# q, k and v of an attention kernel loaded in two transfers each: rows of 1024 and 2048 floats, and the remainders

## The chip, the cores and the metric

The kernel runs on one core of a Trainium2 chip. The metric is device time in microseconds of one launch, as the median of several runs; lower is better.

## The reference

Three layers follow each other: an attention with two sparse masks, a mixture of experts in which 8 experts take 288 tokens each by greedy choice, and a dense block with an elu. Cut to what matters:

```python
def _attn_ref(q, k, v):                       # q, k, v: (4, 8, 576, 64)
    scores = np.matmul(q, k.transpose(0, 1, 3, 2)) / np.sqrt(64)
    rel = pos[:, None] - pos[None, :]         # pos = arange(576)
    mask_local = (rel >= 0) & (rel < 32)
    mask_strided = (rel >= 0) & (pos[None, :] % 32 == pos[:, None] % 32)
    ...                                       # heads 0 to 3 local, 4 to 7 strided
    return np.matmul(softmax(scores), v)

def _moe_ref(x, w_gate, w1, w2):              # x: (2304, 512)
    # the largest logits first, each token to one expert, each expert 288 tokens
    out[mask] = np.maximum(x[mask] @ w1[e], 0) @ w2[e]

def _moe2_ref(x, w_in, w_out):                # w_in, w_out: float64
    return elu(x @ w_in) @ w_out
```

## The kernel before

The host part, `layout`, brings the inputs into the order in which they are loaded. Heads and batches are grouped to 8 units of 1152 queries, and both kinds of mask become blocks of 32 queries by 64 keys.

`attention` goes over the units. For unit u, `load_k` loads `kt` (the transposed keys, with 32 zero columns ahead) in two transfers of 64 partitions each into `kd`, one half for each of two heads, and `qt` in one transfer of 128 partitions; `load_v` loads `vb` in two transfers of 32 partitions into `vd`. `kd`, `vd`, `qt` and the output `os` have two buffers each, so the loads of unit u+2 can start only when unit u has been read, and the output of unit u+2 can be written only when that of unit u is stored. The other halves of `kd` and `vd` are zero (`zero`), so that one matmul works for two heads.

Each unit has three steps. TensorE (PE) computes scores (`s_step`), transposes (`t_step`), multiplies with v (`v_step`), transposes again (`x_step`), and at the end of a unit computes routing logits (`l_step`). VectorE (DVE) and ScalarE (ACT) do the softmax. `store` writes a unit's output to `x_d` in DRAM in four transfers with rows of 512 bytes; the experts gather their tokens from there.

Beside the attention runs the preparation of the dense weights (`Dense.slice`): 16 slices, each loaded as 1 MB of float64 words (`in_wd`), and taken apart by ACT, DVE and GpSimd (POOL).

All loads and stores named so far are issued by SyncE (SP), in program order. That order, and the order of each engine's work, comes from a planner, `Line`, which keeps estimated clocks while the program is written. `line.dma(bytes)` charges a transfer 520 ns of queue time and its bytes at 360 a nanosecond; the result says from when on work that needs it is written, and a dense slice is written in only when the DMA clock is less than 2 us ahead (`DMA_AHEAD`).

After the attention the routing finds the tokens of the first expert, a chain on DVE and PE. Then eight experts, each followed by the dense block, keep PE occupied to the end.

Of the kernel before, what the change touches and what calls it, by code (L numbers as in the profile page):

```python
# [36 lines left out]
ORDER = [0, 1, 2, 3, 4, 5, 6, 9, 10, 11, 12, 7, 8, 13, 14, 15]  # L37


# ---------------------------------------------------------------- host layout  # L40
def layout(inp):
    out = {}

    def rows(a):
        a = a.reshape(B, 2, 2, 2, S, D).transpose(0, 1, 3, 2, 4, 5)
        loc = a[:, 0]
        strided = a[:, 1].reshape(B, 2, 2, 18, 32, D).transpose(0, 1, 2, 4, 3, 5).reshape(B, 2, 2, S, D)
        return np.stack([loc, strided], 1).reshape(8, 2, 2 * S, D)

    qr, kr, vr = rows(inp['q']), rows(inp['k']), rows(inp['v'])  # L50
    out['qt'] = np.ascontiguousarray(qr.transpose(0, 1, 3, 2).reshape(8, 128, 4, 3, 96).transpose(0, 1, 3, 2, 4)).reshape(8, 128, 1152)
    kt = np.zeros((8, 2, D, 1184), np.float32)
    kt[..., 32:] = kr.transpose(0, 1, 3, 2)
    out['kt'] = kt.reshape(8, 128, 1184)
    vb = np.ones((8, 2, 32, 36, 65), np.float32)
    vb[..., :64] = vr.reshape(8, 2, 36, 32, D).transpose(0, 1, 3, 2, 4)
    out['vb'] = vb

    low = np.float32(-8e9)
    masks = np.zeros((128, 2, 9, 64), np.float32)  # L60
    qq, kk = np.arange(32)[:, None], np.arange(64)[None, :]
    for j in range(4):
        for i in range(9):
            b18 = (9 * j + i) % 18
            rk, rq = 32 * b18 - 32 + kk, 32 * b18 + qq
            near = (rk >= 0) & (rq >= rk) & (rq - rk < 32)
            same = (rk >= 0) & (rq >= rk) & (rq // 18 == rk // 18)
            masks[32 * j:32 * j + 32, 0, i] = np.where(near, 0, low)
            masks[32 * j:32 * j + 32, 1, i] = np.where(same, 0, low)
    out['mask'] = masks.astype(ml_dtypes.bfloat16)  # L70

    p, c = np.arange(128)[:, None], np.arange(18)[None]
    flat = 128 * (c // 2) + p
    n = 288 * (c % 2) + flat % 288
    t = 576 * (flat // 288) + 32 * (n % 18) + n // 18
    r = 576 * (flat // 288) + n
    out['tokp'] = np.stack([r // 128, r % 128, t // 128, t % 128], -1).astype(ml_dtypes.bfloat16)
    row = np.zeros((128, 16), np.float32)
    row[:, 0:3] = np.arange(3)
    row[:, 8:16] = 8 - np.arange(8)  # L80
    out['rowc'] = row.astype(ml_dtypes.bfloat16)
    out['ufull'] = np.broadcast_to(np.arange(96, dtype=np.float32)[None, :, None],
                                   (128, 96, 18)).astype(ml_dtypes.bfloat16)
    q = np.arange(128)
    out['tri'] = np.stack([q[:, None] <= q[None], np.ones((128, 128))], 1).astype(np.float32).astype(ml_dtypes.bfloat16)

    w1 = inp['moe_w1'].reshape(8, 4, 128, 8, 128).transpose(0, 3, 2, 1, 4).reshape(8, 8, 128, 512)
    w2 = inp['moe_w2'].reshape(8, 8, 128, 512)
    out['we'] = np.ascontiguousarray(np.concatenate([w1, w2], -1)).reshape(64, 128, 1024)
    wi = inp['moe2_w_in'].reshape(4, 128, 16, 128).transpose(2, 1, 0, 3).reshape(16, 128, 512)  # L90
    wo = inp['moe2_w_out'].reshape(16, 128, 512)
    out['wd'] = np.ascontiguousarray(np.concatenate([wi, wo], -1)).view(np.int64)
    out['wg'] = np.pad(inp['moe_w_gate'].reshape(4, 128, 8).transpose(1, 0, 2), ((0, 0), (0, 0), (0, 24)))
    return out


# ---------------------------------------------------------------- estimated clocks that order the work of the engines
class Line:
    """The tensor engine's program drives an estimated clock; jobs (generators that yield the time of their next piece)
    emit the other engines' work at the estimated time when its operands are there, so that no in-order queue blocks."""  # L100
    LAT = 190

    def __init__(self):
# [61 lines left out]
            self.step(40)  # L165

    def idle(self, eng, cost):
        """Whether the engine is idle and no job that it is urgent for is about to want it."""
        u = min([j[1] for j in self.jobs if eng in j[3]], default=1e18)
        return self.free[eng] <= self.now + 80 and not (self.calm and eng != 'pool') and u > self.now + cost - SLACK  # L170

# [2 lines left out]
            yield max(self.now + 40, min(self.free[eng], self.now + 400))  # L174

    def either(self, n):
        """GpSimd or the vector engine for n columns of a two-operand operation, whichever has room."""
        while True:
            if self.free['pool'] <= self.now + POOL_AHEAD and not self.quiet:
                return 'pool'  # L180
# [3 lines left out]


class Bank:
    """One PSUM bank that several jobs share."""

    def __init__(self, pool, line):
        self.pool, self.line, self.taken, self.at = pool, line, False, 0  # L190
# [8 lines left out]
        self.taken, self.at = False, at  # L199


# ---------------------------------------------------------------- dense weights: float64 words to two float32r parts
class Dense:
    """The 16 slices of the hidden dimension, [128, 512] of w_in and [128, 512] of w_out each, as high and low part:
    RES stay on chip in tiles of their own, as many as there are workers in the workers' tiles, the rest goes as float32
    words by DRAM."""

    def __init__(self, nc, I, dr, pool, early, line):
        self.nc, self.I, self.early, self.late, self.line = nc, I, early, None, line
# [14 lines left out]
        self.left -= 1  # L224

    def slice(self, f, k):
        """Float32 words from the float64 ones, then their high and low part."""
        nc, line = self.nc, self.line
        w = self.pool.tile([128, 2048], U32, name="w64", tag=f"w{k}")
        even, odd = w[:, 0::2], w[:, 1::2].bitcast(F32)  # L230
# [50 lines left out]
        t = 0  # L281
# [10 lines left out]
        self.gfree.append(gk)  # L292

    def keep(self):
        """One more slice stays, in the tiles that the float32 words are worked out in."""
        hi, lo = (self.pool.tile([128, 1024], F32R, name="kept", tag=f"g{x}") for x in range(2))
        self.kept = [(hi[:, 512 * n:512 * n + 512], lo[:, 512 * n:512 * n + 512]) for n in range(2)]


# ---------------------------------------------------------------- attention  # L300
def attention(nc, tc, I, x_d, lg, identf, identb, R, line):
    with ExitStack() as ctx:
        cp = ctx.enter_context(tc.tile_pool(name="ac", bufs=1))
# [7 lines left out]
        def load_k(u):  # L311
            qt = wp.tile([128, 1152], F32, name="qt")
            kd = kd_b[u % 2]
            for x in range(2):
                nc.sync.dma_start(kd[64 * x:64 * x + 64, x, :], I['kt'][u, 64 * x:64 * x + 64])
                line.dma(303104)
            nc.sync.dma_start(qt, I['qt'][u])
            U[u] = dict(qt=qt, kd=kd, tk=line.dma(589824))

        def load_v(u):  # L320
            vd = vd_b[u % 2]
            for x in range(2):
                nc.sync.dma_start(vd[64 * x + 32:64 * x + 64, x, 1:37], I['vb'][u, x])
                t = line.dma(299520)
            U[u].update(vd=vd, tv=[])
            line.add(windows(u, vd, t), 0)

# [20 lines left out]
        def zero(engine, eng, tiles, i, lower):  # L348
            for x in range(2):
# [2 lines left out]
                line.put(eng[x] if isinstance(eng, list) else eng, 1240 if not lower else 2070)  # L352
                if lower:
                    engine.memset(tiles[i][64 * x + 32:64 * x + 64, x, 0], 0.0)

        zero([nc.vector, nc.gpsimd], ['dve', 'pool'], kd_b, 0, False)
        load_k(0)
# [222 lines left out]
        line.finish(last)  # L580


# ---------------------------------------------------------------- greedy routing, one expert filled per phase
COLUMNS = ('lm', 'm', 'eq', 'a8', 'oh', 's', 'w', 'cur', 'cd', 'inE', 'sl', 'x1', 't12', 'u', 'V', 'vp')


class Router:
# [47 lines left out]
        self.line.dve(c1 - c0)  # L635

    def prelude(self, p, c0, c1):
        """Of the tokens in the columns c0 to c1: the best open expert, one-hot, and the digits of its logit."""
        t, line, v, D = self.t, self.line, self.nc.vector, self.line.dve
        n = c1 - c0  # L640
        e8 = self.e8[:, None, :].to_broadcast([128, n, 8])
# [38 lines left out]
        yield e  # L680

    def phase(self, p, res, bank, then=None):
        """Fills res['eidx'] ([1,1] int32, the expert that is filled) and res['idx'] ([96,3,2] int32, their
        rows of x and their tokens)."""
        nc, t, line, n = self.nc, {k: x[:, :self.n] if k in COLUMNS else x for k, x in self.t.items()}, self.line, self.n
        v, D = nc.vector, line.dve

# [155 lines left out]
            yield D(8)  # L843

    def compact(self, bank):
        """Moves the tokens that are left, half as many as there were, to the first half of the columns, in their
        order: one-hot products over the three bfloat16 parts of their logits, which add up to them exactly."""
        nc, line, t = self.nc, self.line, self.t
        v, D = nc.vector, line.dve
        ge = self.ge[:, 0, 18:36]  # L850
# [65 lines left out]
        yield max(e, D(9))  # L916


# ---------------------------------------------------------------- experts and the dense block behind them
class Moe:  # L920
    RING, RAW = 3, 3

# [25 lines left out]
        self.nc.tensor.matmul(out, l, r, **kw)  # L948
        self.line.step(n / 2.4 + 2.6)

    # ---- weights of the experts and streamed dense slices, in the order of their use
    def loader(self, n, stream):
        nc, line, dense = self.nc, self.line, self.dense
        for p in range(8):
# [49 lines left out]
        return w  # L1004

    def warm(self, n):
        """Keeps the tensor engine's clock up while it waits."""
        ps = self.hp.tile([128, 512], F32, name="h")
        for _ in range(n):
            self.nc.tensor.matmul(ps[:96], self.wide[:, :96], self.wide[:, :512], start=True, stop=True)  # L1010

    # ---- tokens of an expert
    def rows_of(self, p, res):
        nc, line = self.nc, self.line
        while 'idx' not in res:
# [31 lines left out]
                self.bank.free(self.x_at + PE_LATE)  # L1047
        self.x_for = p

    # ---- stage 1: relu(x w1) w2  # L1050
    def h_item(self, p, f):
        nc, line = self.nc, self.line
        hi, lo, _ = self.take(('e', p, f, 0))
# [48 lines left out]

        return line.add(evac(), 0)

    # ---- stage 2: elu(y w_in) w_out
    def hin_item(self, ph, N, k, W):
        self.line.hold(lambda: self.y_at[k] is not None)
        self.line.until(self.y_at[k])
# [247 lines left out]
```

## Time and profile before

| what | value |
|---|---|
| median of three runs | 880.23 us (877.32 to 880.27) |
| span of the profiled execution | 880.0 us |
| PE busy | 786.9 us, 89% |
| DVE busy | 551.3 us, 63% |
| ACT busy | 368.4 us, 42% |
| POOL busy | 324.8 us, 37% |
| DMA | 50658 packets, 96.58 MB, mean 110 GB/s |

The page gives each engine's busy time, and the span in 40 slices of 22 us, each digit a busy share in tenths. The attention is the first five of these slices, the routing ahead of the first expert the sixth. The profiled execution's own time is not given apart from its span; the span is 0.2 us below the median.

### The profile page before, as it was taken

To read this page: it belongs to the slowest core of one execution; us is meant where nothing else is said; L and a number is where in the kernel's file an instruction comes from. 1 tells how busy PE (TensorE), PEld (TensorE's weight loads), DVE (VectorE), ACT (ScalarE), POOL (GpSimd) and SP (SyncE) were. 2 spreads that over 40 slices of the span, in tenths; PEclk is the share of its full clock that TensorE was granted. 3 is DMA by queue.
4 is the path that set the end of the run, shared out by engine and by line. 5 is a ranking of instruction groups with operands and counts; after the bars stand their busy time and mean duration, and the time that the engine had idled before them with its cause. 6 is when DMAs were issued, how large, how long until landed. Compare 5 with 4: busy or idle time off the path is not lost. (4 is left out here: it accounts for less than half of the span.)

```text
span 880.0 us, 16883 instructions
## 1 busy us (share of the span) xinstructions
PE 786.9 (89%) x6300; PEld 712.2 (81%) x6300; DVE 551.3 (63%) x1587; ACT 368.4 (42%) x770; POOL 324.8 (37%) x261
## 2 busy tenths in 40 slices
PE   3877844899899789969999999989999999999997
PEld 2656542888789779968999989989998999999896
DVE  4878876999987576678735763178438424533331
ACT  2766822555533332324334422434254345344221
POOL 5141313655535450263226320533174254325101
PEclk9898965888899989989999999989999999999999
DMA  9999627773513620432144122322342423212000
GB/s 211 295 257 284 182 71 163 263 260 114 117 61 120 111 85 14 64 120 74 60 76 145 60 40 25 120 85 96 28 168 96 52 100 110 80 60 85 1 1 36
DMA packets 50658, 96.58 MB, mean 110 GB/s; under 512 B 10256, under 2 KB 19984, under 8 KB 48016
## 3 DMA queue, kind: packets, MB, share of 16 engines
q1 hardware_dynamic: 47600, 86.07, 32.1%
q0 software_dynamic: 2976, 9.44, 7.2%
q8 instruction: 49, 0.80, 0.4%
q14 instruction: 33, 0.27, 0.1%
HBM read 83.94 MB, written 11.54 MB: 109 GB/s over the span
## 5 line engine op out<-in xcount | busy, mean ns | idle before, releaser
L217 POOL TENSOR_TENSOR wl<-raw,wh 128x512 fp32r<-128x512 f32 x161 | 212.4, 1335 | 281.1 <-ACT wh L989 279.6
L989 ACT ACTIVATE wh<-raw 128x512 fp32r<-128x512 f32 x178 | 111.0, 629 | 122.2 <-PE h L948 62.5
L1133 ACT ACTIVATE e<-h 128x256 f32<-128x256 f32 (+2 forms) x130 | 49.5, 390 | 132.6 <-PE h L948 130.2
L1139 ACT ACTIVATE ah<-e 128x256 fp32r<-128x256 f32 (+2 forms) x135 | 56.8, 423 | 111.6 <-DVE e L1137 109.3
L1135 DVE TENSOR_SCALAR e<-e 128x256 f32<-128x256 f32 (+2 forms) x138 | 54.8, 397 | 75.0 <-ACT e L1133 74.2
L1071 DVE SCALAR_TENSOR_TENSOR al<-h,ah 128x288 fp32r<-128x288 f32 x64 | 29.0, 454 | 96.0 <-ACT ah L1069 95.9
L948 PE MATMUL h<-yl,dense_hi 128*128 128x256 f32 (+1 forms) x284 | 86.3, 304 | 3.1 <-DVE yl L1099 3.1
L1141 DVE TENSOR_TENSOR al<-e,ah 128x256 fp32r<-128x256 f32 (+2 forms) x135 | 67.5, 506 | 31.2 <-ACT ah L1139 29.3
L948 PE MATMUL h<-yh,dense_lo 128*128 128x256 f32 (+1 forms) x284 | 86.5, 305 | 0.0
L948 PE MATMUL h<-yh,dense_hi 128*128 128x256 f32 (+1 forms) x284 | 86.3, 304 | 0.0
L948 PE MATMUL yo<-al,wh 128*128 128x288 f32 x256 | 77.4, 302 | 3.2 <-DVE al L1071 3.1
L948 PE MATMUL h<-xh,wh 128*128 128x288 f32 x256 | 76.9, 303 | 0.6 <-ACT xh L1042 0.6
L948 PE MATMUL h<-xh,wl 128*128 128x288 f32 x256 | 77.3, 304 | 0.0
L948 PE MATMUL yo<-ah,wh 128*128 128x288 f32 x256 | 76.8, 300 | 0.0
L948 PE MATMUL yo<-ah,wl 128*128 128x288 f32 x256 | 76.3, 298 | 0.2 <-POOL wl L217 0.2
L948 PE MATMUL h<-xl,wh 128*128 128x288 f32 x256 | 73.3, 301 | 0.0
L740 PE MATMUL pc<-r_ohU,r_oh 128*128 128x31 bf16 (+1 forms) x594 | 52.7, 255 | 16.5 <-DVE r_ohU L711 11.6
L217 POOL TENSOR_TENSOR g<-g,w 128x512 f32<-128x512 f32 x24 | 35.9, 1504 | 82.3 <-DVE g L253 39.3
L948 PE MATMUL yo<-dense_hi,al 128*128 128x512 f32 x156 | 63.8, 409 | 1.0 <-DVE al L1141 0.9
L948 PE MATMUL yo<-dense_lo,ah 128*128 128x512 f32 x156 | 62.5, 400 | 0.0
L740 PEld LDWEIGHTS <-r_oh 128*128 128x128 bf16 x594 | 44.6, 117 | 22.0 <-issue 17.7
L948 PE MATMUL yo<-dense_hi,ah 128*128 128x512 f32 x156 | 62.2, 398 | 0.0
(240 smaller groups left out, 2039.0 us busy)
## 6 DMA issues: line engine op xcount, KB each, us to landing
raw<-in_we SPq DMA_DIRECT2D x128, 256.0 KB, 2.7
w<-in_wd SPq DMA_DIRECT2D x16, 1024.0 KB, 6.6
raw<-dense_words SPq DMA_DIRECT2D x52, 256.0 KB, 3.0
kd<-in_kt SPq DMA_DIRECT2D x16, 296.0 KB, 8.1
vd<-in_vb SPq DMA_DIRECT2D x16, 292.5 KB, 10.8
qt<-in_qt SPq DMA_DIRECT2D x8, 576.0 KB, 7.8
x_d<-os SPq DMA_DIRECT2D x32, 144.0 KB, 6.3
dense_words<-g SPq DMA_DIRECT2D x4, 512.0 KB
```

The lines of the kernel that those rows point to most:

```text
L217: (self.nc.vector if eng == 'dve' else self.nc.gpsimd).tensor_tensor(*a, **kw)
L740: nc.tensor.matmul(pc[:, :K], t['oh'][:, c, :], t['cmp'][:, :K, c], start=(c == 0), stop=(c == n - 1))
L948: self.nc.tensor.matmul(out, l, r, **kw)
L989: nc.scalar.activation(hi, r, AF.Copy)
L1071: nc.vector.scalar_tensor_tensor(al, ph, 0.0, ah.bitcast(F32), op0=OP.max, op1=OP.subtract)
L1133: nc.scalar.activation(e, x, AF.Exp)
L1135: nc.vector.tensor_scalar(e, e, 1.0, -1.0, op0=OP.min, op1=OP.add)
L1139: nc.scalar.activation(h, e, AF.Copy)
L1141: nc.vector.tensor_tensor(l, e, h.bitcast(F32), op=OP.subtract)
```

## The change

The rows of `kt` lose their zero columns. `qt`, `kt` and `vb` are cut into an array with the first 1024 (`qt`, `kt`) or 2048 (`vb`) floats of each row, and one with the rest (`qtr`, `ktr`, `vbr`: 128, 128 and 292 floats). Each load becomes two. The zero columns are written on the chip by one small memset for each half of each `kd` buffer. The planner is told of each transfer. Comments and docstrings are removed elsewhere, which shifts line numbers: what stands on lines 315, 317, 323 and 234 before stands on 318, 322, 331 and 236 now.

```diff
-    kt = np.zeros((8, 2, D, 1184), np.float32)
-    kt[..., 32:] = kr.transpose(0, 1, 3, 2)
-    out['kt'] = kt.reshape(8, 128, 1184)
+    def cut(name, a, n):
+
+        out[name], out[name + 'r'] = np.ascontiguousarray(a[..., :n]), np.ascontiguousarray(a[..., n:])
+
+    cut('qt', qr.transpose(0, 1, 3, 2).reshape(8, 128, 4, 3, 96).transpose(0, 1, 3, 2, 4).reshape(8, 128, 1152), 1024)
+    cut('kt', kr.transpose(0, 1, 3, 2).reshape(8, 128, 1152), 1024)
...
-    out['vb'] = vb
+    cut('vb', vb.reshape(8, 2, 32, 2340), 2048)
...
             for x in range(2):
-                nc.sync.dma_start(kd[64 * x:64 * x + 64, x, :], I['kt'][u, 64 * x:64 * x + 64])
-                line.dma(303104)
-            nc.sync.dma_start(qt, I['qt'][u])
-            U[u] = dict(qt=qt, kd=kd, tk=line.dma(589824))
+                h = slice(64 * x, 64 * x + 64)
+                nc.sync.dma_start(kd[h, x, 32:1056], I['kt'][u, h])
+                line.dma(262144)
+                nc.sync.dma_start(kd[h, x, 1056:], I['ktr'][u, h])
+                line.dma(32768)
+            nc.sync.dma_start(qt[:, :1024], I['qt'][u])
+            line.dma(524288)
+            nc.sync.dma_start(qt[:, 1024:], I['qtr'][u])
+            U[u] = dict(qt=qt, kd=kd, tk=line.dma(65536))
...
             for x in range(2):
-                nc.sync.dma_start(vd[64 * x + 32:64 * x + 64, x, 1:37], I['vb'][u, x])
-                t = line.dma(299520)
+                d = vd[64 * x + 32:64 * x + 64, x, 1:37].rearrange("p c d -> p (c d)")
+                nc.sync.dma_start(d[:, :2048], I['vb'][u, x])
+                line.dma(262144)
+                nc.sync.dma_start(d[:, 2048:], I['vbr'][u, x])
+                t = line.dma(37376)
...
                 if lower:
                     engine.memset(tiles[i][64 * x + 32:64 * x + 64, x, 0], 0.0)
+                else:
+                    (engine[x] if isinstance(engine, list) else engine).memset(tiles[i][64 * x:64 * x + 64, x, 0:32], 0.0)
```

How the order moves. On SP, from unit 2's loads on (`kd0` and `kd1` are the two buffers of `kd`, `w64` holds the words of a dense slice; the brackets name the semaphores that a transfer waits for, and DMAHW0 to DMAHW7 are those that SP's transfers signal in turn). Before:

```order
L315 DMA kd0_128<-in_kt 64x1184 [waits DMAHW5_49,PE_49]
L315 DMA kd0_128<-in_kt 64x1184 [waits DMAHW6_49]
L317 DMA qt_230<-in_qt 128x1152 [waits DMAHW7_49]
L234 DMA w64_174<-in_wd 128x2048 [waits DMAHW0_49]
L234 DMA w64_175<-in_wd 128x2048 [waits DMAHW1_49]
L315 DMA kd1_129<-in_kt 64x1184 [waits DMAHW2_49,PE_49]
L315 DMA kd1_129<-in_kt 64x1184 [waits DMAHW3_49]
L317 DMA qt_357<-in_qt 128x1152 [waits DMAHW4_49]
```

On SP at the same place in the changed kernel:

```order
L318 DMA kd0_128<-in_kt 64x1024 [waits DMAHW7_49,PE_49]
L320 DMA kd0_128<-in_ktr 64x128 [waits DMAHW0_49,PE_49]
L318 DMA kd0_128<-in_kt 64x1024 [waits DMAHW1_49]
L320 DMA kd0_128<-in_ktr 64x128 [waits DMAHW2_49]
L322 DMA qt_244<-in_qt 128x1024 [waits DMAHW3_49]
L324 DMA qt_244<-in_qtr 128x128 [waits DMAHW4_49]
L236 DMA w64_188<-in_wd 128x2048 [waits DMAHW5_49]
L318 DMA kd1_129<-in_kt 64x1024 [waits DMAHW6_49,PE_49]
```

One dense slice instead of two stands ahead of unit 3's loads, and unit 2's first transfer waits for DMAHW7 where it waited for DMAHW5. The second slice stands further back on SP in the changed kernel, behind unit 3's `qt` and unit 2's `vd`:

```order
L324 DMA qt_373<-in_qtr 128x128 [waits DMAHW3_49]
L331 DMA vd0_130<-in_vb 32x2048 [waits DVE_49,DMAHW4_49,PE_49,Activation_49]
L333 DMA vd0_130<-in_vbr 32x292 [waits DMAHW5_49,PE_49]
L331 DMA vd0_130<-in_vb 32x2048 [waits DMAHW6_49,DVE_49]
L333 DMA vd0_130<-in_vbr 32x292 [waits DMAHW7_49]
L236 DMA w64_189<-in_wd 128x2048 [waits DMAHW0_49]
L318 DMA kd0_128<-in_kt 64x1024 [waits DMAHW1_49,PE_49]
```

From the third slice on, the slices stand where they stood among the loads; a ninth one is loaded ahead of the first expert's weights, where there were eight.

## Rows read from the trace of the kernel before

**Rows 1.** The page: span, and DMA share in 40 slices, in tenths.

```profile
span 880.0 us, 16883 instructions
...
DMA  9999627773513620432144122322342423212000
```

**Rows 2.** Stretches: length, busy us of PE, PEld, DVE, ACT, POOL; PEclk, DMA share, GB/s.

```profile
50.00:60.00 10.00, 6.23 (x122) 4.49 (x121) 5.09 (x13) 6.42 (x13) 3.90 (x3) 1.00 1.01 254
...
250.00:300.00 50.00, 49.61 (x430) 47.65 (x428) 36.53 (x133) 18.18 (x44) 25.69 (x21) 1.00 0.34 93
```

**Rows 3.** Waits, 0 to 112 us: who waited for what, total us, times, longest.

```profile
PE ps L394 <- DMA qt<-in_qt: 12.6, 2, 9.8
...
DVE os L462 <- DMA x_d<-os: 7.1, 3, 4.8
...
PE po L447 <- DVE os L462: 3.1, 2, 2.4
```

**Rows 4.** Timeline, PE and DVE: start, us, instruction, [idle before, releaser].

```profile
6.21 1.04 DVE L351 MEMSET kd<- 64x1184 f32 x1 [0.28 <-issue]
...
9.81 1.50 PE L394 MATMUL ps<-kd,qt 128*32 128x128 f32 x24 [9.81 <-DMA qt<-in_qt]
...
39.15 1.06 PE L394 MATMUL ps<-kd,qt 128*32 128x128 f32 x24 [2.79 <-DMA qt<-in_qt]
...
59.56 0.56 DVE L462 TENSOR_TENSOR os<-po,r 128x384 f32<-128x384 f32 x1 [4.75 <-DMA x_d<-os]
...
60.27 1.53 PE L447 MATMUL po<-vd,pts 128*32 128x130 f32 x24 [2.43 <-DVE os L462]
...
80.78 0.56 DVE L462 TENSOR_TENSOR os<-po,r 128x384 f32<-128x384 f32 x1 [1.69 <-DMA x_d<-os]
...
114.80 2.23 PE L740 MATMUL pc<-r_ohU,r_oh 128*128 128x63 bf16 x18 [2.90 <-DVE r_ohU L711]
```

**Rows 5.** Stretches in which mostly one kind of load moves (columns as in rows 2).

```profile
25.00:28.00 3.00, 3.00 (x63) 2.24 (x65) 2.24 (x7) 1.86 (x4) 0.00 (x0) 0.83 1.02 426
61.00:62.00 1.00, 1.00 (x25) 1.00 (x21) 0.93 (x4) 0.72 (x2) 0.00 (x0) 0.50 0.99 277
...
64.00:65.00 1.00, 1.00 (x12) 0.39 (x11) 0.97 (x3) 1.00 (x2) 1.00 (x1) 1.00 0.67 264
74.00:75.00 1.00, 0.01 (x1) 0.00 (x0) 1.00 (x1) 0.97 (x2) 1.00 (x2) 1.00 0.92 189
90.00:91.00 1.00, 1.00 (x27) 0.83 (x31) 0.97 (x2) 0.98 (x2) 0.68 (x1) 1.00 1.21 290
```

**Rows 6.** The tile kd: issues on SP and memsets, ns min/median/max, first and last start.

```profile
L315 SPq DMA_DIRECT2D kd<-in_kt x16: 471/526/597, 0.8 to 70.5; - x16
L351 DVE MEMSET kd<- x3: 1045/1045/1045, 1.1 to 6.2; 64x1184 f32 x3
```

**Rows 7.** The page, DMA issues: count, KB each, median us from issue to landing.

```profile
raw<-in_we SPq DMA_DIRECT2D x128, 256.0 KB, 2.7
...
kd<-in_kt SPq DMA_DIRECT2D x16, 296.0 KB, 8.1
vd<-in_vb SPq DMA_DIRECT2D x16, 292.5 KB, 10.8
qt<-in_qt SPq DMA_DIRECT2D x8, 576.0 KB, 7.8
```

**Rows 8.** Timeline of SP, DMA issues: start, us, instruction, count.

```profile
15.12 1.22 SPq L315 DMA_DIRECT2D kd<-in_kt  x2
...
18.70 0.96 SPq L234 DMA_DIRECT2D w<-in_wd  x2
27.34 1.11 SPq L315 DMA_DIRECT2D kd<-in_kt  x2
...
48.98 2.26 SPq L480 DMA_DIRECT2D x_d<-os  x4
```

**Rows 9.** DMA packets between 104 and 105 us, stores of x_d alone (share 0.98).

```profile
DMA packets 477, 0.23 MB, mean 229 GB/s; under 512 B 30, under 2 KB 477, under 8 KB 477
```

More of the change, by code (lines that the diff above doesn't have):

```diff
@@ L50, in layout @@
     qr, kr, vr = rows(inp['q']), rows(inp['k']), rows(inp['v'])
-    out['qt'] = np.ascontiguousarray(qr.transpose(0, 1, 3, 2).reshape(8, 128, 4, 3, 96).transpose(0, 1, 3, 2, 4)).reshape(8, 128, 1152)
-    kt = np.zeros((8, 2, D, 1184), np.float32)
-    kt[..., 32:] = kr.transpose(0, 1, 3, 2)
-    out['kt'] = kt.reshape(8, 128, 1184)
+    def cut(name, a, n):
+        out[name], out[name + 'r'] = np.ascontiguousarray(a[..., :n]), np.ascontiguousarray(a[..., n:])
+    cut('qt', qr.transpose(0, 1, 3, 2).reshape(8, 128, 4, 3, 96).transpose(0, 1, 3, 2, 4).reshape(8, 128, 1152), 1024)
+    cut('kt', kr.transpose(0, 1, 3, 2).reshape(8, 128, 1152), 1024)
     vb = np.ones((8, 2, 32, 36, 65), np.float32)
     vb[..., :64] = vr.reshape(8, 2, 36, 32, D).transpose(0, 1, 3, 2, 4)
-    out['vb'] = vb
+    cut('vb', vb.reshape(8, 2, 32, 2340), 2048)
     low = np.float32(-8e9)
```

## The prediction

> **What bounds the kernel now.** The page first: the row "DMA" [rows 1] gives the DMA engines' busy share in slices of 22 us. The first four read 9, the later ones mostly 1 to 6. The table of stretches [rows 2] says the same of the engines: between 50 and 60 us PE is busy 6.23 of 10 us while the DMA share is 1.01; between 250 and 300 us PE is busy 49.61 of 50 and DMA 0.34. So q, k and v are loaded in the one stage where DMA is full and PE is not, and nothing gained or lost there is hidden later: PE fills the rest.
>
> The table of waits [rows 3] names what reaches PE: 12.6 us on `qt` in two waits, and 7.1 us of DVE on the stores of `x_d`, which PE feels as 3.1 us. In time order [rows 4]: the first matmul starts at 9.81; at 39.15 PE has waited 2.79 us for the `qt` of unit 3; at 59.56 DVE has waited 4.75 us for the stores of unit 1 (unit 3 writes the same `os` buffer), so PE resumes only at 60.27; at 80.78 DVE waits 1.69 us again, for unit 3's.
>
> Are the loads slow by their rows? Rates stand in the stretches of [rows 5]; GB/s over share is the rate at a full engine. Dense slices alone (8192-byte rows): 426/1.02 = 418. `qt` alone (4608-byte rows): 264/0.67 = 394. `kd` (4736-byte rows): 189/0.92 = 205 at 74 us, but 277/0.99 = 280 at 61 us with the same rows. A row of 4608 bytes is as fast as one of 8192, and one of 4736 is slow only at times. What sets `kd` and `vd` apart is that they reach 64 and 32 partitions, and this change leaves that as it is. So I expect the rates to stay.
>
> **The change, part by part.**
>
> *More transfers.* 16 `kd`, 8 `qt` and 16 `vd` loads become 80: 40 more. On SP a `kd` issue costs 526 ns [rows 6].
>
> *Eight in flight.* In the order shown above, SP's transfers rotate over eight semaphores, and each waits for the eighth before it. Before, eight loads in a row are four of `kd`, two of `vd`, two of `qt`: 4x296 + 2x292.5 + 2x576 = 2921 KB [rows 7]. Now eight transfers carry half, 1460 KB. At 230 GB/s, between the 205 and 280 above, that is 6.5 us of work. A 256 KB load lands after 2.7 us [rows 7], of which 0.6 is moving at 418 GB/s, so 2.1 us are fixed. 6.5 us cover this. Below: nothing. Above: each eight must land before the next, 40/8 x 2.1 = 10.5 us. I take **+0.7**, near the lower end, since the cover is three times the need.
>
> *Start.* Three more issues stand before the first unit's last part, 3 x 0.53 = 1.6 us at most; nothing at least, since `qt`'s data follows `kd`'s on the same engines, which need 606 KB at 205 GB/s, 3 us, for `kd`. I take 0.6, nearer to nothing; it delays the loads behind it, counted next.
>
> *A dense slice changes places.* This is the largest piece. The planner charges 520 ns of queue time for each transfer, so its DMA clock runs later. Before, both slices were issued at 18.70, ahead of unit 3's loads [rows 8]; now one is, and the other stands behind unit 3's `kd`, `qt` and unit 2's `vd`. Also, unit 2's first `kd` was issued at 15.12, and now waits for the semaphore of the second `vd` load, which the first slice waited for before: it cannot start much before 18.70. In the stretch from 25 to 28 us DMA moves almost only the two slices, at 426 GB/s [rows 5], so they end about when unit 3's load is issued, at 27.34. With one slice DMA runs dry 2.5 us earlier (1.05 MB at 426 GB/s), and starts again with unit 3's load, which waits for the last scores of unit 1 and so is late by the start's 0.6.
>
> First, that is a gain: unit 3's load has no second slice ahead of it, and the 2.79 us wait at 39.15 shrinks or goes. What is late next is the wait at 59.56. The stores of unit 1, issued at 48.98, stand behind all DMA work since 28: three units' k and q, two of v, unit 0's stores and now two slices instead of one. In a full queue their landing moves by the work: the slice, 2.5 us; the restart, 0.6 us; and more packets. Each of three units of k and q has 256 more, each of two of v 64: 896. A stretch of 512-byte rows has 477 packets at share 0.98 in 1 us [rows 9], 32.9 ns each, of which 512 bytes at 418/16 GB/s are 19.6: 13 ns each, 896 x 13 / 16 = 0.7 us. Sum **+3.8 us** at 60.27, in place of the start's term and unit 3's gain, not beside them. Below: 0, if the queue has air that I don't see. Above: 5.
>
> *Later stores.* Unit 3's stores are issued behind unit 7's loads, which have three more issues, 1.6 us; DVE already waits for them at 80.78. Between 0 and 1.6 I take **+0.8**, the middle, since PE's own wait there is for other work as well. The packets of the remaining loads, 2x256 + 4x64 = 768, are 0.6 us; half of it on the path, **+0.3**.
>
> *Small edits.* The zero columns of `kt` are no longer loaded: 32x4x1024 bytes = 131 KB, 0.3 us at 418 GB/s, a third on the path: -0.1. Four memsets of 64x32 are added; one of 64x1184 takes 1045 ns [rows 6]. By columns one of the new costs 0.03 us, by its being an instruction up to 1.05. DVE has three of them and its last memset ends at 7.25, 2.5 us before the first matmul, which waits for its load; so up to 0.8 us each are hidden: 0. Without that cover, at 1.05 each, 0.6 us.
>
> *The stages behind.* PE's order is unchanged up to expert 0; there a few of the router's matmuls stand two to four rows away, and one dense slice more is loaded before the routing. I take 0, between -3 (a slice less to load beside the first expert) and +3 (dense work late on DVE).
>
> Sum: 3.8 + 0.7 + 0.8 + 0.3 - 0.1 = 5.5. The profiled span is 880.0 [rows 1], 0.2 below the median of the runs, 880.23: **885.5 us**. A measurement of this kernel tells about 0.5% from no change, 4.4 us.
>
> **Rivals.**
>
> *Rows that run faster (the other side).* If the odd rows were what is slow, `kd` would go from 205 to 418 GB/s: 16 x 303 KB = 4.85 MB, 23.7 to 11.6 us of full DMA. `vd` (4.79 MB) goes at 290/1.21 = 240 GB/s at 90 us [rows 5], and would give up 8.5 us. Of these 20 us PE can take what it loses to loads and stores: 2.79 + 3.1, and half of the first load, some 1.5: -7.5, so 872.5. It decides if `kd`'s rate at a full engine rises to 350 or more. Against: 280 at 61 us with the old rows, and `qt`. Chance 0.13. [...]
>
> *The cover breaks.* Eight small transfers don't hide the fixed 2.1 us, and SP issues in the rhythm of landings: +10.5 in place of 0.7, 895. For: landings of 7.8 to 10.8 us [rows 7] already hold SP back by those semaphores. Against: 6.5 us of work. Chance 0.15. [...]
>
> *The slice's move is free.* The queue has air before unit 1's stores, so they land when they did, and unit 3's gain pays for the start: 880.0 + 0.8 + 0.7 = 881.5. For: at 64 us DMA is at 0.67 [rows 5]. Against: share 1.01 between 50 and 60. Chance 0.22.
>
> **How the numbers follow.** Forecast 0.50 (own range 881 to 891). Slower by over 0.5% (above 884.6): 0.37 of the forecast and 0.15 of the broken cover, 0.52. Faster (below 875.8): 0.11 of faster rows, 0.03 of the free move, 0.14. Within: the rest, 0.34. The range runs from 877 to 894: it leaves out most of the faster rows and the upper half of the broken cover.
>
> **What would show it.** Right: `kd` still near 205 to 280 GB/s; the wait for unit 3's `qt` under 1 us; the wait of DVE for unit 1's stores ending near 63; the first routing matmul (before at 114.80 [rows 4]) some 5 us later; the stretch behind it as long as before. Wrong: that wait ending by 60, a `kd` rate over 350, or a difference that arises behind the routing.

## The result and the profile after

| | before | with the change |
|---|---|---|
| median of 4 runs, us | 880.25 (877.32 to 884.23) | 892.10 (890.78 to 895.54) |
| ratio of the runs, 95% interval | | 1.0147 (1.0109 to 1.0186) |
| profiled execution: span, its own time, us | 880.0, 880.23 | 891.4, 893.21 |

The change makes the kernel 1.5% slower, by 11.9 us in the medians and 11.4 in the spans. The page of the profile after shows the same outline as [rows 1]; the loads, which are parts now, land sooner than in [rows 7]:

```profile
span 891.4 us, 16961 instructions
...
DMA  8999746664622460251335113142242423212000
...
kd<-in_kt SPq DMA_DIRECT2D x16, 256.0 KB, 5.5
qt<-in_qt SPq DMA_DIRECT2D x8, 512.0 KB, 6.5
vd<-in_vb SPq DMA_DIRECT2D x16, 256.0 KB, 5.7
```

The waits from 0 to 112 us answer to [rows 3]; SPq's rows are waits of SP's queue:

```profile
DVE os L474 <- DMA x_d<-os: 17.5, 5, 8.0
...
SPq L492 <- DMA w<-in_wd: 10.2, 3, 3.7
PE ps L406 <- DMA qt<-in_qt: 9.6, 2, 9.0
...
PE po L459 <- DVE os L474: 6.0, 2, 4.1
```

PE waits for `qt` 3 us less, DVE waits for the stores of `x_d` 17.5 us in place of 7.1. In time order (PE and DVE, as in [rows 4]):

```profile
8.96 1.51 PE L406 MATMUL ps<-kd,qt 128*32 128x128 f32 x24 [8.96 <-DMA qt<-in_qt]
...
49.72 0.56 DVE L474 TENSOR_TENSOR os<-po,r 128x384 f32<-128x384 f32 x1 [7.96 <-DMA x_d<-os]
50.42 0.88 PE L459 MATMUL po<-vd,pts 128*32 128x130 f32 x12 [4.08 <-DVE os L474]
...
62.64 0.56 DVE L474 TENSOR_TENSOR os<-po,r 128x384 f32<-128x384 f32 x1 [1.38 <-DMA x_d<-os]
63.35 1.01 PE L459 MATMUL po<-vd,pts 128*32 128x130 f32 x17 [2.02 <-DVE r L470]
...
119.89 1.31 PE L752 MATMUL pc<-r_ohU,r_oh 128*128 128x63 bf16 x10 [2.89 <-DVE r_ohU L723]
```

The wait for unit 3's `qt` is gone. A wait of 7.96 us for the stores of unit 0, one unit earlier than the one foreseen, takes the lead. The work of DMA around it, before and after (columns as in [rows 2]):

```profile
27.00:32.00 5.00, 5.00 (x122) 4.00 (x111) 4.55 (x13) 3.57 (x7) 0.00 (x0) 1.00 0.98 287
```

```profile
27.00:32.00 5.00, 5.00 (x114) 4.21 (x112) 4.54 (x12) 3.90 (x8) 0.00 (x0) 1.00 0.62 150
32.00:48.00 16.00, 11.19 (x231) 8.11 (x228) 7.62 (x20) 11.14 (x20) 4.22 (x3) 1.00 1.00 253
```

SP's timeline of the change, and for the first two of the four parts of unit 0's store the time from issue to landing:

```profile
32.83 0.49 SPq L236 DMA_DIRECT2D w<-in_wd  x1
...
39.94 6.13 SPq L492 DMA_DIRECT2D x_d<-os  x4
...
x_d<-os SPq DMA_DIRECT2D x1, 144.0 KB, 8.3
x_d<-os SPq DMA_DIRECT2D x1, 144.0 KB, 4.6
```

With one slice in place of two, DMA runs dry between 27 and 32 us (share 0.62 in place of 0.98), and the second slice, issued at 32.83, then stands ahead of unit 0's store in a queue that is full up to 48 us. The four parts of the store also take long to issue, 6.13 us (4.44 in before): SP's eight semaphores have turned round to that of the slice, and parts of stores wait 10.2 us in all for dense slices (`w<-in_wd`) to land. But this hold is not what makes the store land late. Its first part, issued at 39.94 ahead of the hold, takes 8.3 us to land; the second, held until 44.07, takes 4.6; both are there at 48.3 to 48.7. The first routing matmul comes at 119.89, 5.1 us after [rows 4].

Then the loss goes on. Expert 0's first matmul (`h<-x`, line 960) starts at 162.28 (before 154.74: +7.5), expert 1's at 271.53 (254.93: +16.6), expert 2's at 368.97 (357.62: +11.4); it is 12.8 at experts 3 and 4, and 11.4 again from there to the end. So 9 us are lost while expert 0 and its dense block run, and 5 come back with expert 1. The stretch of expert 0, from its first matmul to expert 1's, before and after (columns as in [rows 2]):

```profile
154.70:254.90 100.20, 90.04 (x625) 83.53 (x626) 97.64 (x222) 53.89 (x100) 57.48 (x39) 0.89 0.54 173
```

```profile
162.20:271.50 109.30, 91.60 (x625) 84.08 (x626) 99.25 (x233) 53.71 (x100) 52.35 (x37) 0.89 0.48 147
```

PE does the same 625 matmuls in 91.6 instead of 90.0 us, at the same mean granted clock of 0.89, and is idle 17.7 instead of 10.2. PE's waits in this stretch of the change that are not in before, or longer there (before: on `px` 1.9 us for `rows` and 1.2 for `xl`, none on `parts`, `pc` 0.8 on `r_ohU` and 2.2 on `r_di`):

```profile
PE px L1050 <- DMA rows<-x_d,r_iall: 5.2, 1, 5.2
PE h L960 <- ACT parts L281: 4.7, 1, 4.7
PE pc L752 <- DVE r_ohU L723: 4.1, 3, 2.9
PE h L960 <- POOL parts L219: 1.3, 1, 1.3
```

`parts` are the last dense slices, made ready on ACT, DVE and POOL (`Dense.slice`) just before expert 0's dense block uses them. The rows of the tile `parts` on ACT, before and after (count, ns min/median/max, first and last start):

```profile
L279 ACT ACTIVATE parts<-g x3: 1051/1059/1060, 217.4 to 246.3; 128x1024 fp32r<-128x1024 f32 x3
```

```profile
L281 ACT ACTIVATE parts<-g x3: 1047/1052/1056, 234.8 to 260.9; 128x1024 fp32r<-128x1024 f32 x3
```

The last comes 91.6 us after expert 0's start before (246.3 - 154.7), 98.6 after it now (260.9 - 162.3). PE reaches the last of them at 257.3 and stands; the stop shows in stretches of 10 us of the change (PE alone: busy, granted clock, DMA share, GB/s), the second with the clock after it:

```profile
252.00:262.00 10.00, 5.28 (x34) 0.98 0.17 54
262.00:272.00 10.00, 8.71 (x40) 0.68 0.00 1
```

Before, PE is busy 10.00 of 10 us from 244 to 254, at a granted clock of 1.00.

### The profile page after: what moved, and what is told of

Its sections match the earlier page's. It is cut to its first block, busy times and chain, and to the rows that moved or that the text cites. A ratio compares the mean times of both kernels' runs of the same rounds, so it can differ in the third digit from the quotient of the medians.

```text
span 891.4 us, 16961 instructions
## 1 busy us (share of the span) xinstructions
PE 782.7 (88%) x6300; PEld 707.6 (79%) x6300; DVE 548.2 (61%) x1593; ACT 370.9 (42%) x772; POOL 316.0 (35%) x257
## 5 line engine op out<-in xcount | busy, mean ns | idle before, releaser
L1145 ACT ACTIVATE e<-h 128x256 f32<-128x256 f32 (+2 forms) x130 | 49.7, 390 | 134.7 <-PE h L960 131.6
L1147 DVE TENSOR_SCALAR e<-e 128x256 f32<-128x256 f32 (+2 forms) x138 | 59.1, 428 | 73.9 <-ACT e L1145 73.4
L1153 DVE TENSOR_TENSOR al<-e,ah 128x256 fp32r<-128x256 f32 (+2 forms) x135 | 70.9, 531 | 31.3 <-ACT ah L1151 29.8
L1149 DVE TENSOR_TENSOR e<-e,h 128x256 f32<-128x256 f32 (+2 forms) x130 | 56.1, 431 | 5.6 <-PE h L960 0.5
```

The costliest lines, as they stand in the source:

```text
L1145: nc.scalar.activation(e, x, AF.Exp)
L1147: nc.vector.tensor_scalar(e, e, 1.0, -1.0, op0=OP.min, op1=OP.add)
L1149: nc.vector.tensor_tensor(e, e, x, op=OP.max)
L1153: nc.vector.tensor_tensor(l, e, h.bitcast(F32), op=OP.subtract)
```

## The experiments

The change does three things at once: loads in two transfers, new arrays, and, through the planner's 520 ns per transfer, another order of all queues. The kernels below take them apart. The 67 runs of the kernel before that stood beside the change and these kernels lie between 877.3 and 890.7 us, and its profiled run of 880.2 is among the shorter ones; so the ratios decide, and single profiles only where the difference is many us or recurs in several kernels. How far single profiles scatter is seen in the seven that keep the old order with the slice where it was on SP (before, e1, e3, e4, e9, e10, e11): their first routing matmul comes between 110.28 and 118.19 us.

**Order and transfers, each alone.** e1 splits the loads and charges the planner as before (each pair once, no queue time for the remainder): apart from the remainders' own instructions all engines keep the old order.

```diff
 nc.sync.dma_start(kd[h, x, 32:1056], I['kt'][u, h])
-line.dma(262144)
 nc.sync.dma_start(kd[h, x, 1056:], I['ktr'][u, h])
-line.dma(32768)
+line.dma(303104)
...
```

> All loads split as in the change, but the planner is told of one transfer each as before, so every engine's order is that of the kernel before. If the moved order is what costs (dense slices and dense work at other places), this is within 3 us of the kernel before, 880 to 883. If the transfers themselves cost (eight in flight, stores that wait for a semaphore that a large load holds), it keeps most of the 11 us: 888 to 893. Unit 3's wait for qt (2.79 us before) should then be there again, since two slices stand ahead of it.

Measured: 881.88 us beside 885.45, ratio 0.996 (0.9937 to 0.9984). Run again (e11):

> The split loads in the old order once more, on this chip. If the gain of its first measurement is real: ratio 0.993 to 0.999 again. If it was that chip's: 1.000 or more.

Measured: 882.43 beside 885.30, ratio 0.9987 (0.9948 to 1.0025). So the gain isn't established; that the split in the old order costs less than 0.3% is.

e2 is the reverse: whole loads of before, the planner charged as the change does.

```diff
 nc.sync.dma_start(kd[64 * x:64 * x + 64, x, :], I['kt'][u, 64 * x:64 * x + 64])
-line.dma(303104)
+line.dma(262144)
+line.dma(32768)
...
```

> Loads whole as before, but the planner is charged for two transfers each, so the order is that of the changed kernel. If the order costs, 888 to 893. If the transfers cost, 880 to 883, and less where unit 3's wait for qt is gone. In the trace: does DVE still wait 7.96 us for unit 0's stores, and does PE still wait 4.74 us for the parts of a dense slice in expert 0's dense block? The first belongs to the transfers if it goes here, the second to the order if it stays.

Measured: 901.11 beside 885.45, ratio 1.0172 (1.0131 to 1.0213); the time lies above the 888 to 893 that I gave, the ratio at the change's. The moved order alone costs what the change costs. But e2 does not lose it in the attention: its first routing matmul comes at 113.93. Its stretch of expert 0 is 112.9 us long.

**Where the order costs.** On SP the order differs up to the routing in one row: the second dense slice. So a two by two can be made. e6 is e1 with that one transfer issued where the change has it; e5 is the change with that one transfer issued where it was. All else stands as in e1 and in the change.

```diff
 # e5, in Dense.slice
+while f == ORDER[1] and not self.first:
+    yield line.now + 1
+if f == ORDER[1]:
+    nc.sync.dma_start(w, self.I['wd'][f].bitcast(U32))
 while line.free['dma'] > line.now + ...
 # e6, in Dense.slice; issue_held() issues it when the planner's time for its landing has come
+t = line.dma(1 << 20)
+if f == ORDER[1]:
+    self.held = (w, f)
...
```

> The change, with one row of SP moved back: the transfer of the second dense slice is issued right behind the first, as before; every other instruction of every engine stands where the change put it. Theory (two separate costs: the slice's place costs the attention its 5 us, the new order of the dense work on DVE, ACT and POOL costs the stretch behind it): the first routing matmul comes at 112 to 115 us, as in the run with the old order (113.5), and the stretch behind it stays longer than before by 6 us or more; ratio 1.007 to 1.018. Rival (the slice's place is the whole cost, the later loss follows from the late attention): ratio 0.995 to 1.002.

> The loads split as in the change, every instruction of every engine in the old order, but for one row of SP: the second dense slice's transfer stands behind unit 3's q and k and unit 2's v, as in the change. Theory (two separate costs): the first routing matmul comes some 5 us later than with the old order, at 117 to 120 us, and the stretch behind it is as long as before within 2 us; ratio 1.001 to 1.006. Rival (the slice's place is the whole cost): ratio 1.012 or more. Rival (the slice's place costs nothing by itself): 0.994 to 0.999.

| slice, other engines | kernel | ratio (95%) | first routing matmul | expert 0's stretch | end against before's profile |
|---|---|---|---|---|---|
| early, old | e1 | 0.996 (0.9937 to 0.9984) | 113.49 | 102.5 | -1.9 |
| late, old | e6 | 1.0036 (1.0007 to 1.0065) | 118.96 | 101.5 | +1.1 |
| early, new | e5 | 1.0116 (1.0047 to 1.0185) | 115.93 | 111.4 | +8.5 |
| late, new | the change | 1.0147 (1.0109 to 1.0186) | 119.89 | 109.3 | +11.4 |

The last column is the start of the last expert's last `h<-x` matmul. The order of the other engines, with SP's rows behind the routing, costs 10.4 us (8.5 + 1.9) or 10.3 (11.4 - 1.1) at the end; 8.9 (111.4 - 102.5) or 7.8 (109.3 - 101.5) of it arise in expert 0's stretch. That stretch is 100.2 to 104.1 us in all nine profiles with the old order and 109.3 to 114.2 in all five with a new one (before and the change among them), and by the ratios e5 lies clear of e1 and the change of e6.

The slice's place costs 5.5 us (118.96 - 113.49) or 4.0 (119.89 - 115.93) at the routing, and 3.0 or 2.9 at the end. This is not firm. These are single profiles: e11, the same kernel as e1, has 115.49, a stretch of 104.1 and +0.7 at the end, and against it the order costs 7.8 us and the slice 0.3. e2, with the slice late as well, comes to the routing at 113.93. By the ratios the slice costs 0.8% (e6 against e1) or 0.5% (against e11, whose interval overlaps e6's), and 0.3% in the new order, where they overlap too. e5's 115.93 also lies above the 112 to 115 given for it. Rows of e6 and of e5, the stretch and SP's store of unit 0, in e6 with a wait of ACT and one of PE:

```profile
158.50:260.00 101.50, 91.86 (x625) 85.41 (x626) 99.10 (x224) 54.37 (x101) 57.46 (x39) 0.87 0.56 174
...
37.18 5.59 SPq L502 DMA_DIRECT2D x_d<-os  x4
...
40.96 1.12 ACT L251 ACTIVATE g<-w 128x1024 f32<-128x1024 f32 x1 [7.98 <-DMA w<-in_wd]
...
42.89 0.69 PE L516 MATMUL px<-identf,os 128*128 128x128 f32 x2 [7.96 <-ACT xt L526]
```

```profile
156.30:267.80 111.50, 92.66 (x625) 85.06 (x626) 99.37 (x233) 53.56 (x100) 52.41 (x37) 0.86 0.49 147
...
40.43 2.21 SPq L499 DMA_DIRECT2D x_d<-os  x4
```

Of these four kernels, those with the slice late issue the store in 5.59 us (e6) and 6.13, those with it early in 2.21, whatever the other engines' order. But in e6 DVE does not wait for that store. ACT there takes the slice apart where the old order has it, ahead of its next work on the attention; the slice lands at 40.9, ACT has waited 7.98 us for it, and PE then 7.96 for ACT. So the late slice delays the attention in both orders, in each by another wait, and the like 3.0 and 2.9 us are no proof of one cost. What stands of the theory is that the order of the other engines costs the later stretch by itself; the rival that the late attention causes the later loss falls, since e6 is as late at the routing and loses nothing in expert 0's stretch.

**The semaphore or the bytes.** e7 issues the change's second slice four rows further down, still ahead of unit 0's stores.

```diff
 for x in range(2):
     ...
+line.issue_held()
 nc.sync.dma_start(qt[:, :1024], I['qt'][u])
```

> The change, with the second dense slice's transfer four rows further down on SP, behind unit 4's k: the transfer that waits for its semaphore, eight rows on, is then a load of v and no longer a part of unit 0's stores. Theory (the store is late because SP waits for the slice's semaphore): the four parts of unit 0's store are issued within 3 us of each other (5.7 us in the change), DVE's longest wait for stores falls from 8.0 us to below 5, and the first routing matmul comes at 115 to 118 us in place of 119.9. Rival (the slice's bytes ahead of the stores in the DMA engines make them late, whatever the semaphore): the wait stays at 7 to 9 us and the matmul at 119 to 121. The stretch behind is that of the change either way.

Measured: ratio 1.0131 (1.0061 to 1.0202); the store, and DVE's wait for it:

```profile
37.24 2.42 SPq L506 DMA_DIRECT2D x_d<-os  x4
...
45.52 0.56 DVE L488 TENSOR_TENSOR os<-po,r 128x384 f32<-128x384 f32 x1 [6.35 <-DMA x_d<-os]
```

The store is issued in 2.42 us, the wait ends at 45.5 in place of 49.7, and the first routing matmul comes at 114.21, sooner than either forecast. The wait itself, 6.35, is above the 5 that I gave. This does not show the semaphore as the cause: e7's execution was ahead before the moved row, with unit 3's first load issued at 24.62 where the change has 26.90, and that is 2.3 of the 4.2 us. And e2, with the slice late and whole loads, has the long wait without the hold (store, its first part's time to landing, DVE's wait):

```profile
33.87 2.62 SPq L483 DMA_DIRECT2D x_d<-os  x4
...
x_d<-os SPq DMA_DIRECT2D x1, 144.0 KB, 10.8
...
45.94 0.56 DVE L465 TENSOR_TENSOR os<-po,r 128x384 f32<-128x384 f32 x1 [7.57 <-DMA x_d<-os]
```

So the rival, the bytes ahead, accounts for the late store; whether the hold adds anything to it no run shows. e7's ratio can't be told from the change's.

e8 takes the slices off SP's semaphores: the old order with the split loads, slices issued by POOL.

```diff
-nc.sync.dma_start(w, self.I['wd'][f].bitcast(U32))
+nc.gpsimd.dma_start(w, self.I['wd'][f].bitcast(U32))
```

> The loads split as in the change, the old order, and all 16 dense slices issued by POOL in place of SP, at the same place of the plan, so that SP's eight semaphores turn among loads and stores alone. Theory (SP's waits for a slice's semaphore cost the attention something in the old order too): DVE's waits for stores fall from 10.0 us in all to below 6 and the first routing matmul comes 1 to 4 us before 113.5; ratio 0.989 to 0.996. Rival (POOL issues slowly or too early, the slices meet the loads): ratio 0.997 to 1.01.

Measured: ratio 1.0136 (1.0067 to 1.0205). My theory fell. POOL issues the first two slices 6 us sooner than SP did [rows 8], and the loads then meet them:

```profile
12.59 1.31 POOL L236 DMA_DIRECT2D w<-in_wd  x2
...
PE ps L403 <- DMA qt<-in_qt: 13.3, 3, 8.5
```

The first routing matmul comes at 127.47; DVE's waits for stores are 18.0 us, 12.09 of them at 96.73, after POOL had issued two more slices at 81.68 beside those stores. On SP the slices stand in one order with the loads and take their turn of the semaphores; I take that to have kept them apart, but no run shows it alone.

**A third plan.** e12 is the change with a longer look-ahead of the planner for dense slices, which puts the ninth slice back behind the gather of expert 0 and leaves the last preparations on ACT where the change has them.

```diff
-DMA_AHEAD = 2000
+DMA_AHEAD = 2400
```

> The change with the planner's look-ahead for dense slices at 2400 ns in place of 2000. The slice in the attention stays behind unit 3's loads; the ninth slice, which the change issues before the gather of expert 0, goes back behind it; the last two preparations on ACT (parts) stay at the change's rows, 5 or 6 rows later than in the old order. Theory (PE waits in expert 0's dense block since the last slices are prepared late): the waits for parts stay at 4 to 7 us, and the stretch from expert 0's first matmul to expert 1's stays at 108 to 113 us (100 to 103 with the old order); ratio 1.010 to 1.018. Rival (the ninth slice's early place is the cause): the stretch is 100 to 104 us, ratio 1.002 to 1.007.

Measured: 895.56, ratio 1.0147 (1.0076 to 1.0217); the stretch is 114.2 us, a little above the 108 to 113 given (the profile is of the longest of its four runs, 901.96), and PE waits there for

```profile
PE h L960 <- ACT parts L281: 4.9, 1, 4.9
...
PE h L960 <- POOL parts L219: 1.3, 1, 1.3
```

So the loss doesn't need the ninth slice's early place. The waits for `parts` are 6.0 to 6.2 us in all five profiles with a new order, and none of the nine with the old one has any. In the change they are 6.0 of the 9.1 us by which expert 0's stretch grew; 1.6 are longer busy time of PE and 1.5 other waits. That `parts` comes late is read from the traces: no run moved its preparation alone, so which of the moved rows makes it late is not shown.

**The rows themselves.** e3 is the kernel before with the rows of `kt` and `vb` padded in DRAM to multiples of 256 bytes; e4 writes the zero columns of `kt` by memsets and doesn't load them.

```diff
 # e3
-kt = np.zeros((8, 2, D, 1184), np.float32)
+kt = np.zeros((8, 2, D, 1216), np.float32)
...
-nc.sync.dma_start(kd[64 * x:64 * x + 64, x, :], I['kt'][u, 64 * x:64 * x + 64])
+nc.sync.dma_start(kd[64 * x:64 * x + 64, x, :], I['kt'][u, 64 * x:64 * x + 64, :1184])
...
 # e4
+nc.sync.dma_start(kd[64 * x:64 * x + 64, x, 32:], I['kt'][u, 64 * x:64 * x + 64])
...
```

> The kernel before, only with rows of kt and vb padded in DRAM to multiples of 256 bytes (1216 and 2368 floats apart); the same bytes are moved by the same transfers. If starts off 256 bytes made the loads slow, kd's stretch at 74 us goes from 205 GB/s at a full engine towards 400 and the time falls by 3 to 8 us, to 872 to 877. If the partitions set the rate, nothing moves: 879 to 882.

> The kernel before without the zero columns in kt: they are written by the four small memsets, and each kd load moves rows of 1152 floats. One part of the change alone. Both theories expect no difference that can be measured, 879 to 882: 131 KB less is 0.3 us of DMA, and the memsets are hidden under the first load.

Measured: e3 0.9964 (0.9927 to 1.0002), e4 0.9982 (0.9954 to 1.0009): neither can be told from no change. In e3 `kd` moves as before; the stretch that answers to 74:75 in [rows 5] has 196 GB/s at share 0.92:

```profile
74.00:75.00 1.00, 0.45 (x3) 0.21 (x3) 0.97 (x2) 0.97 (x2) 1.00 (x1) 1.00 0.92 196
```

**Transfers or arrays.** Expert 1's stretch (`h<-x` of expert 1 to that of expert 2) fell into two groups that have nothing to do with the order: 97 to 99 us with the new arrays, 103 to 106 without. e9 issues two transfers out of the one old array; e10 is the kernel before with three more arrays that nothing reads.

```diff
 # e9
-nc.sync.dma_start(qt, I['qt'][u])
+nc.sync.dma_start(qt[:, :1024], I['qt'][u, :, :1024])
+nc.sync.dma_start(qt[:, 1024:], I['qt'][u, :, 1024:])
...
 # e10, in layout
+for n, c, k in (('qtr', 128, 128), ('ktr', 128, 128), ('vbr', 64, 292)):
+    out[n] = np.zeros((8, c, k), np.float32)
```

> The kernel before, its arrays and its order, each load of q, k and v issued as two transfers out of the one array (no arrays of remainders, the planner charged as before). In all runs so far the wait for the gathered rows of expert 2, at 305 us, was 4.4 to 6 us with whole loads and 1 us or less with split ones. If the number of transfers is what matters: that wait 1 us or less, ratio 0.994 to 0.999. If the new arrays are (where the tensors lie in memory): that wait 4 us or more, ratio 0.998 to 1.004.

> The kernel before, with three more input arrays of the shapes of the remainders, which nothing reads. If the number of transfers is what shortens the wait at 305 us: the wait stays at 4 us or more, ratio 0.998 to 1.002. If the new arrays are: 1 us or less, ratio 0.994 to 0.999.

Measured: e9 1.0061 (1.0019 to 1.0103), above both ratios that I gave, expert 1's stretch 103.8; e10 0.9973 (0.9936 to 1.001), expert 1's stretch 98.0. The wait for expert 2's gathered rows goes with the arrays, even if nothing reads them; rows of before and of e10 around it (landing times of the weights and of the gather, and PE's wait):

```profile
raw<-in_we SPq DMA_DIRECT2D x2, 256.0 KB, 12.1
rows<-x_d,r_iall POOLq DMA_INDIRECT x3, 12.2
...
PE px L1038 <- DMA rows<-x_d,r_iall: 4.4, 1, 4.4
```

```profile
raw<-in_we SPq DMA_DIRECT2D x4, 256.0 KB, 6.6
rows<-x_d,r_iall POOLq DMA_INDIRECT x3, 10.6
...
PE px L1040 <- DMA rows<-x_d,r_iall: 0.8, 1, 0.8
```

All nine profiles with the three arrays show a wait of 1.2 us or less there, all five without one of 3.7 us or more. What the arrays change (where `x_d` or the weights then lie in memory would be one way) was not tried. And the split out of one array is slower by 0.2 to 1.0%, so splitting is not free everywhere. Whether the new arrays pay for it in the change is not shown: e10's gain is within the noise, and e9 also reads its remainders at another spacing in DRAM, as parts of the old rows.

No kernel here is shown to beat the kernel before; e1, the split in the old order, is at 0.996 and 0.9987 in two measurements.

## Why the prediction was right in sign and range, and wrong in the sum

The forecast was 885.5 with a range to 894; 892.1 lies in it. That is luck in part: 5.3 us more were forecast and 11.9 came, the forecast's own range ended at 891, and the rest of the range stood there for the broken cover, which did not come. Step by step:

- *A dense slice changes places, +3.8 at 60.27.* Right in the main: DMA ran dry, the slice's bytes stood ahead of the stores, the unit-3 wait went, the same step of PE starts at 63.35, +3.1, and the first routing matmul at 119.89, +5.1, where "some 5 us later" was forecast (a mark that scatters by 8 us among kernels with the slice where it was). DVE's wait for unit 1's stores ends at 62.64, where 63 was given; what I missed is that unit 0's store, behind the same bytes, would be waited for first. And of the 4.0 to 5.5 us at the routing, 3 at most reach the end (e5, e6; 0.3 against e11); I took all of it through.
- *Start, +0.6.* Not seen: the first matmul starts at 8.96, 0.85 sooner, but single profiles start between 8.4 and 9.8 with whole loads and between 7.9 and 9.1 with split ones.
- *Later stores, +0.8 and +0.3.* No run separates them. DVE's waits for stores behind 63 us are 3.39, 3.35 and 1.46 in the change, where before has 1.69. The queue of loads and stores moved 3200 packets more, where the rows cut in two are 2560; the other 640 are 16 for each of the 40 new transfers, and I had not counted those.
- *Eight in flight, +0.7 (0 to 10.5).* Too small, if e9 stands for it: its 0.61% are 5.4 us (1.7 to 9.1), inside the bounds. Together with the new arrays it is nothing that could be measured (e1, e11). The Trainium skill, "DMA: Bandwidth & Descriptors", section "Rules for kernel authors", wants small transfers joined; e9's interval agrees with that, e1's 0.996 and 0.9987 do not show it.
- *The stages behind, 0, between -3 and +3.* **This is the step that failed.** I looked at PE's order alone and gave "dense work late on DVE" 3 us at most. The new order of the engines costs 10.4 us at the end (e5 against e1; 7.8 against e11), and 6 us of it are PE's stop for the late `parts` in expert 0's dense block. The sign that I named for being wrong, a difference that arises behind the routing, is what came.
- *Rows and rates.* Right: in the change DMA moves 168 GB/s at share 0.85, that is 198, from 45 to 47 us, where `kd`'s loads land; padded rows change nothing that could be measured (e3); faster rows are no rival. *Zero columns, memsets:* right within the measurement (e4).
- *Sum.* What was measured, by the profiles: split and arrays in the old order -1.9, the slice's place +3.0, the other engines' order +10.3, sum +11.4; with e11 for e1, +0.7, +0.3 and +10.3. Mine: +5.5, with the slice at 3.8 and the order at 0.

The rival "the cover breaks" would have given 895, nearer than the forecast, and for the wrong reason: e1 has the same transfers and is not slower.

## What to carry to other kernels

Where a planner orders the queues by estimated costs, an edit of the loads is also an edit of its clock: diff the order on every engine, follow the work that is prepared late to whoever uses it, and test the edit once with the planner's charges held as they were. In a queue whose transfers take a fixed number of semaphores in turn, a large load holds up the issue of the transfer that takes its semaphore next; before you call that the cause of a late landing, look when a part that was issued ahead of the hold has landed. Two kernels that lose about the same at one mark need not lose it by the same wait, so read the waits of each. A delay in one stage reaches the end only in part; carry each term to the last stage, not to the next mark.

## What the runs showed of the hardware that was not expected

DVE's work ahead of the last `parts` of the change takes longer beside POOL's. Between 255 and 259 us (DVE, then POOL):

```profile
256.00 1.52 DVE L1153 TENSOR_TENSOR al<-e,ah 128x256 fp32r<-128x256 f32 x1
257.44 1.36 DVE L1147 TENSOR_SCALAR e<-e 128x256 f32<-128x256 f32 x1
...
255.46 1.78 POOL L219 TENSOR_TENSOR wl<-raw,wh 128x512 fp32r<-128x512 f32 x1 [1.64 <-ACT wh L1001]
257.20 1.46 POOL L219 TENSOR_TENSOR g<-g,w 128x512 f32<-128x512 f32 x1
```

The same two DVE instructions take 0.42 us (at 259.78) and 0.28 us (at 254.02) when POOL is idle; here each ends 0.1 to 0.3 us after POOL's. That is 1.10 + 1.08 us of delay for DVE just ahead of the last `parts`. Before has such a case too: `al` takes 1.51 us at 248.01, beside an operation of POOL from 247.45 to 249.25; so the delay by itself is no difference between the two kernels. The Trainium skill, "SBUF — State Buffer", section "SBUF: two separate sides", says that GpSimd's operations and certain DVE operations share a pair of ports as an exclusive lock, held for the whole instruction by the one that starts first; these rows agree.

Three unused arrays, 1.6 MB in all, go with a wait for a gather 300 us into the kernel that is some 4 us shorter. A change of the inputs' layout can so move a stage that it has nothing to do with, and half a per cent is then no proof of the edit itself.
